# An attention, 2-D DFT and MLP kernel: the DFT as 6- and 4-point elementwise DFTs with small tile DFTs behind them, and the three stages of different batches interleaved by a hand-written dispatcher

## The chip, the core and the metric

One Trainium2 chip, one of its cores. The metric is device time in microseconds of one execution. The core has five engines that run in parallel, each through its own instructions in order: PE (matrix products, with weight loads, PEld, beside them), DVE (vector), ACT (activations), POOL (GpSimd) and SP, which here only issues DMAs. PE writes to PSUM, eight banks of 2 KB a partition; everything else lies in SBUF (128 partitions) or in DRAM.

## The reference

```python
# q, k, v: (4, 8, 768, 64) f32; n_global = 8, n_local = 96; w_ch1: (512, 2048); w_ch2: (2048, 512)
scores = matmul(q, k.T) / sqrt(64)                   # per batch and head
keep = (key < n_global) | (0 <= query - key < n_local)
dist = n_local where a global key is not local, else |query - key|
scores = where(keep, scores - slope[head] * dist, -1e9)
x = softmax(scores) @ v                              # -> (4, 768, 512), the heads side by side
u = x + real(fft2(x))                                # over the sequence (768) and the channels (512)
un = (u - mean(u)) / sqrt(var(u) + 1e-6)             # over the channels
out = u + maximum(un @ w_ch1, 0) @ w_ch2
```

## The kernel before

A batch is 768 rows of 512 channels, so six tiles of 128 rows. The work of one batch has three stages, in f16 with f32 sums:

- `attention(b, hp)`, for a pair of heads: six DMAs bring q, k, v (`qsb`, `ksb`, `vsb`; 192 KB each, in rows of 256 bytes) in f32. ACT casts q and v, DVE casts k. PE transposes q and k tile by tile (`ptq`, `ptk`), DVE copies each (`qT`, `kT`). For each head and each tile of 128 keys, PE makes the scores `pss` (keys on partitions; 768 queries for the first tile, since its first 8 keys are seen by all, 256 for the others), ACT takes exp to `eraw`, and DVE multiplies by a mask in f16, `b0m` or `bgm`, which holds the exponentials of the distance and zeros, and which DMAs bring. For each tile of queries, PE sums up to three products (`pav`) with v and a column of ones, DVE takes the reciprocal of the last column (`rcol`), and ACT or DVE scales to `xn`.
- `mix(b)`, first part: the DFT over the sequence as a full product with cosine and sine matrices (`csm`, `ssm`): for four tiles of channels and two matrices, six products of 512 columns to `pm`; DVE copies (`yt`) and fills the last 256 columns by symmetry. Then the DFT over the channels: for each of six row tiles, eight products of 512 columns to `pmx`. DVE adds `xn` to give `u` and takes its statistics (`st`, `mvall`); after the sixth tile ACT and DVE make one `rstd` for all; DVE normalises (`un`), PE transposes (`ptu`), DVE copies (`unT`).
- `mix(b)`, second part, the MLP, in two halves of 384 rows: 16 times four products to `ph`, with the relu on ACT (`hT`); then for three row tiles 16 products of 512 columns to `pg`; DVE adds `u` (`ob`), a DMA writes it.

The weights come in f32 through a single staging buffer each (`w1tmp`, `w2tmp`), and DVE casts them. The order is that of the program at its end: attention of batch 0, the loads of constants and weights, and then for each batch the attention of the next one and the mix of this one. A scheduler orders the instructions on each engine by their data and their buffers, with that order as the priority; the pools (`bufs`) set how far a stage runs ahead. PSUM is split into three banks for attention, three for mix and MLP, two for transposes.

Of the kernel before, what the change touches and what calls it, by code (L numbers as in the profile page):

```python
# [9 lines left out]
FP16 = mybir.dt.float16  # L11
# [4 lines left out]
P = 128  # L16

CAST_E = "scalar"
MASK_E = "gpsimd"
# [3 lines left out]
def kernel(  # L23
# [19 lines left out]
    HP = H // 2  # L43

    hsl = np.arange(H, dtype=np.float64)
    slopes = 2.0 ** (-8.0 * (hsl + 1) / H)

    kk = np.arange(P)[:, None]
    qq = np.arange(256)[None, :]
    rel_g = qq - kk  # L50
    in_band_g = (rel_g >= 0) & (rel_g < NL)
    Bgen = np.zeros((H, P, 256))
    for h in range(H):
        Bgen[h] = np.where(in_band_g, np.exp(-slopes[h] * rel_g), 0.0)
    qa = np.arange(S)[None, :]
    rel0 = qa - kk
    in_band0 = (rel0 >= 0) & (rel0 < NL)
    is_g = kk < NG
    dist0 = np.where(in_band0, rel0, NL)
    B0 = np.zeros((H, P, S))  # L60
    for h in range(H):
        loc = np.where(in_band0, np.exp(-slopes[h] * rel0), 0.0)
        glob = np.exp(-slopes[h] * dist0)
        B0[h] = np.where(is_g, glob, np.where(kk >= NG, loc, 0.0))
    b0_d = nc.inline_tensor(B0.astype(np.float16), name="b0m")
    bg_d = nc.inline_tensor(Bgen.astype(np.float16), name="bgm")

    ii = np.arange(S)
    ang_s = 2.0 * np.pi * np.outer(ii % S, ii) / S
    CS = np.cos(ang_s)  # L70
    SSm = np.sin(ang_s)
    ddi = np.arange(Dm)
    ang_d = 2.0 * np.pi * np.outer(ddi, ddi) / Dm
    CD = np.cos(ang_d)
    SDn = -np.sin(ang_d)
    cs_d = nc.inline_tensor(CS.astype(np.float16), name="csm")
    ss_d = nc.inline_tensor(SSm.astype(np.float16), name="ssm")
    cd_d = nc.inline_tensor(CD.astype(np.float16), name="cdm")
    sd_d = nc.inline_tensor(SDn.astype(np.float16), name="sdm")
    id_d = nc.inline_tensor(np.eye(P, dtype=np.float16), name="idm")  # L80

    konst = ctx.enter_context(tc.tile_pool(name="konst", bufs=1))
    att = ctx.enter_context(tc.tile_pool(name="att", bufs=2))
    att1 = ctx.enter_context(tc.tile_pool(name="att1", bufs=2))
    mixp = ctx.enter_context(tc.tile_pool(name="mixp", bufs=1))
    up = ctx.enter_context(tc.tile_pool(name="up", bufs=1))
    outp = ctx.enter_context(tc.tile_pool(name="outp", bufs=2))
    xnp = ctx.enter_context(tc.tile_pool(name="xnp", bufs=2))
    small = ctx.enter_context(tc.tile_pool(name="small", bufs=12))
    ps = ctx.enter_context(tc.tile_pool(name="ps", bufs=3, space=bass.MemoryType.PSUM))  # L90
    psm = ctx.enter_context(tc.tile_pool(name="psm", bufs=3, space=bass.MemoryType.PSUM))
    pst = ctx.enter_context(tc.tile_pool(name="pst", bufs=2, space=bass.MemoryType.PSUM))

    def cast_op(o, i, scale=None):
        if CAST_E == "scalar":
            if scale is None:
                nc.scalar.activation(o, i, AF.Copy)
            else:
                nc.scalar.activation(o, i, AF.Copy, 0.0, scale)
        else:  # L100
            if scale is None:
                nc.vector.tensor_copy(o, i)
            else:
                nc.vector.tensor_scalar_mul(o, i, scale)

    mask_ctr = [0]

    def mask_op(o, a, bm):
        eng = nc.gpsimd if (mask_ctr[0] % 2 == 0) else nc.vector
        mask_ctr[0] += 1  # L110
        eng.tensor_tensor(o, a, bm, op=ALU.mult)

    ident = konst.tile([P, P], FP16, tag="ident", name="ident")
    nc.sync.dma_start(ident, id_d.ap())
    epsc = konst.tile([P, 1], FP32, tag="epsc", name="epsc")
    nc.vector.memset(epsc, 1e-6)
    b0_sb = []
    bg_sb = []
    for h in range(H):
        t1 = konst.tile([P, S], FP16, tag=f"b0_{h}", name=f"b0_{h}")  # L120
        nc.sync.dma_start(t1, b0_d.ap()[h])
        b0_sb.append(t1)
        t2 = konst.tile([P, 256], FP16, tag=f"bg_{h}", name=f"bg_{h}")
        nc.sync.dma_start(t2, bg_d.ap()[h])
        bg_sb.append(t2)
    cs_sb = []
    ss_sb = []
    cd_sb = []
    sd_sb = []
    w1f = []  # L130
    w2f = []

    def load_big_consts():
      for a in range(NS):
          t1 = konst.tile([P, S], FP16, tag=f"cs{a}", name=f"cs{a}")
          nc.sync.dma_start(t1, cs_d.ap()[a * P:(a + 1) * P, :])
          cs_sb.append(t1)
          t2 = konst.tile([P, S], FP16, tag=f"ss{a}", name=f"ss{a}")
          nc.sync.dma_start(t2, ss_d.ap()[a * P:(a + 1) * P, :])
          ss_sb.append(t2)  # L140
      for a in range(ND):
          t1 = konst.tile([P, Dm], FP16, tag=f"cd{a}", name=f"cd{a}")
          nc.sync.dma_start(t1, cd_d.ap()[a * P:(a + 1) * P, :])
          cd_sb.append(t1)
# [219 lines left out]
```

## Time and profile before

| | |
|---|---|
| time, median of 3 runs | 450.07 us (449.8 to 451.08) |
| span of the profiled execution, its own time | 452.1 us |
| PE busy | 390.5 us, 86% of the span |
| DVE, ACT, POOL busy | 242.2, 199.5, 0.2 us |
| mean granted clock of PE | 0.913 |
| DMA | 39.52 MB, mean 87 GB/s |

The span runs from the first to the last instruction of one execution. Busy times of PE hold pipelined matmuls and overlap themselves. A group's row gives: line, engine, operation, out<-in, its shape and count | busy us, mean ns of one | idle time of the engine just before them, and what ended it. A row of the chain in order of time gives start, duration and what ran. In a row by stretches stand the stretch, its length, the busy time and count of PE, PEld, DVE, ACT and POOL, the granted clock, the share of the DMA engines, and GB/s.

### The profile page before, as it was taken

The numbers are of one execution on the slowest core, as the hardware profiler recorded it, in microseconds if no ns is written. First come the engines' busy times: TensorE is split into PE (matmuls) and PEld (weight loads), VectorE is DVE, ScalarE is ACT, GpSimd is POOL, SyncE is SP. The second block draws the span as 40 slices with busy tenths as digits, with TensorE's granted clock in tenths as the row PEclk, the third lists the DMA queues.
The fourth block names the chain that finished last, engine by engine and source line by source line (L and its number), as shares of the span: only waits on it lengthen the run. The fifth ranks groups of instructions, "written<-read, shape, count | busy, mean of one in ns | idle before, by whom it ended". The sixth has DMA issues, their size and how long they took to land.

```text
span 452.1 us, 6542 instructions
## 1 busy us (share of the span) xinstructions
PE 390.5 (86%) x2272; PEld 190.2 (42%) x2272; DVE 242.2 (54%) x1029; ACT 199.5 (44%) x506; POOL 0.2 (0%) x4
## 2 busy tenths in 40 slices
PE   0488989957889999999769999999589999959996
PEld 0133334323345454444335454444255554435452
DVE  0377678989872104898970104999950105871101
ACT  1377451548666150786716160776424330006060
POOL 0000000000000000000000000000000000000000
PEclk9999989955559999998959999999969999979999
DMA  7999318887799101362340101000000101000101
GB/s 205 223 223 304 78 35 225 250 222 195 175 199 164 70 1 70 71 129 56 81 88 0 71 0 71 0 3 1 1 0 7 65 25 46 1 0 1 60 11 71
DMA packets 87537, 39.52 MB, mean 87 GB/s; under 512 B 76752, under 2 KB 81360, under 8 KB 87504
## 3 DMA queue, kind: packets, MB, share of 16 engines
q1 hardware_dynamic: 87504, 39.10, 35.0%
q8 instruction: 18, 0.29, 0.3%
q14 instruction: 15, 0.12, 0.1%
HBM read 32.80 MB, written 6.29 MB: 86 GB/s over the span
## 4 chain that ended last, share of the span: by engine, by line
PE 73%; DVE 13%; DMA 7%; ACT 3%; issue 2%; SPq 1%; DVEq 0%; ACTq 0%
PE ph L306 20%; PE pg L315 18%; PE pm L261 9%; PE pmx L279 8%; PE pss L224 5%; PE pss L213 3%; PE pav L240 3%; DMA w2tmp<-in_moe_w_ch_dram 3%; PE ptk L197 2%; DVE un L292 2%; DMA w1tmp<-in_moe_w_ch_dram 2%; PE ptq L194 2%; PE ptu L297 2%; DVE rcol L243 2%; DVE expst L228 2%
## 5 line engine op out<-in xcount | busy, mean ns | idle before, releaser
L310 ACT ACTIVATE hT<-ph 128x384 f16<-128x384 f32 x128 | 62.7, 490 | 89.2 <-PE ph L306 87.9
L306 PE MATMUL ph<-unT,w1f 128*128 128x384 f16 x512 | 97.0, 344 | 0.0
L318 DVE TENSOR_TENSOR ob<-pg,u 128x512 f32<-128x512 f32 x24 | 16.6, 691 | 142.0 <-PE pg L315 142.0
L315 PE MATMUL pg<-w2f,hT 128*128 128x512 f16 x384 | 84.2, 379 | 0.0
L306 PEld LDWEIGHTS <-w1f 128*128 128x128 f16 x512 | 52.0, 102 | 39.4 <-issue 9.1
L315 PEld LDWEIGHTS <-hT 128*128 128x128 f16 x384 | 37.6, 98 | 44.4
L227 ACT ACTIVATE eraw<-pss 128x256 f16<-128x256 f32 (+1 forms) x160 | 49.0, 369 | 5.8 <-PE pss L224 4.1
L217 ACT ACTIVATE eraw<-pss 128x384 f16<-128x384 f32 x64 | 29.8, 489 | 46.6 <-PE pss L213 46.2
L240 PE MATMUL pav<-v,expst 128*128 128x65 f16 x480 | 41.7, 212 | 9.4 <-ACT xn L245 4.6
L240 PEld LDWEIGHTS <-expst 128*128 128x128 f16 x480 | 32.0, 108 | 29.8 <-issue 12.4
L224 PE MATMUL pss<-qT,kT 64*128 64x256 f16 (+1 forms) x160 | 41.5, 307 | 2.1 <-ACT eraw L217 1.3
L245 ACT ACTIVATE xn<-pav,rcol 128x64 f16<-128x64 f32 x96 | 28.7, 311 | 31.3 <-DVE rcol L243 30.7
L297 PE MATMUL ptu<-ident,un 128*128 128x128 f16 x96 | 24.2, 280 | 18.5 <-DVE un L292 13.6
L194 PE MATMUL ptq<-ident,q 128*128 128x128 f16 x96 | 24.0, 250 | 18.5 <-ACT q L181 16.8
L228 DVE TENSOR_TENSOR expst<-eraw,bg 128x256 f16<-128x256 f16 (+1 forms) x160 | 36.4, 272 | 4.4 <-ACT eraw L227 3.1
L261 PE MATMUL pm<-cs,xn 128*128 128x512 f16 x96 | 30.3, 416 | 0.0
L243 DVE RECIPROCAL rcol<-pav 128x1 f32<-128x1 f32 x192 | 26.5, 161 | 6.8 <-PE pav L240 4.3
L197 PE MATMUL ptk<-ident,k 128*128 128x128 f16 x96 | 23.8, 248 | 6.5 <-DVE kT L198 5.5
L279 PE MATMUL pmx<-sd,yt 128*128 128x512 f16 x96 | 29.2, 385 | 0.0
L279 PE MATMUL pmx<-cd,yt 128*128 128x512 f16 x96 | 28.8, 391 | 0.0
L261 PE MATMUL pm<-ss,xn 128*128 128x512 f16 x96 | 26.6, 385 | 0.8 <-DVE yt L265 0.8
L188 ACT ACTIVATE v<-vsb 128x384 f16<-128x384 f32 x32 | 16.7, 521 | 22.8 <-DMA vsb<-in_v_dram 18.3
(35 smaller groups left out, 337.8 us busy)
## 6 DMA issues: line engine op xcount, KB each, us to landing
qsb<-in_q_dram SPq DMA_DIRECT2D x32, 192.0 KB, 4.1
ksb<-in_k_dram SPq DMA_DIRECT2D x32, 192.0 KB, 4.2
vsb<-in_v_dram SPq DMA_DIRECT2D x32, 192.0 KB, 4.2
out_dram<-ob SPq DMA_DIRECT2D x24, 256.0 KB, 2.0
w1tmp<-in_moe_w_ch_dram SPq DMA_DIRECT2D x8, 512.0 KB, 4.3
w2tmp<-in_moe_w_ch_dram SPq DMA_DIRECT2D x16, 256.0 KB, 3.4
b<-b0m SPq DMA_DIRECT2D x8, 192.0 KB, 3.5
cs<-csm SPq DMA_DIRECT2D x6, 192.0 KB, 4.0
```

The source lines that it names most:

```text
L194: nc.tensor.transpose(pt, q16[:, i * P:(i + 1) * P], ident)
L224: nc.tensor.matmul(pss, kT[hb:hb + Dh, i * P:(i + 1) * P], qT[hb:hb + Dh, qlo:qlo + w], start=True, stop=True)
L227: nc.scalar.activation(eraw[:, ecol(i):ecol(i) + w], pss, AF.Exp)
L228: nc.vector.tensor_tensor(expst[:, ecol(i):ecol(i) + w], eraw[:, ecol(i):ecol(i) + w], bg_sb[h][:, 0:w], op=ALU.mult)
L240: nc.tensor.matmul(pav[:, 0:65], lhsT, v16b[hslot][:, kb, 0:65], start=(t == 0), stop=(t == n - 1))
L243: nc.vector.reciprocal(rcol, pav[:, 64:65])
L261: nc.tensor.matmul(pm, xn[b][si][:, dc * P:(dc + 1) * P], kon[si][:, 0:512], start=(si == 0), stop=(si == NS - 1))
L279: nc.tensor.matmul(pm, yt[(ch, di)][:, j * P:(j + 1) * P], kon2[di], start=(t == 0), stop=(t == 2 * ND - 1))
L297: nc.tensor.transpose(ptu, un16t[j][:, dc * P:(dc + 1) * P], ident)
L306: nc.tensor.matmul(ph, w1f[di][:, jb * P:(jb + 1) * P], unTt[di][:, half * 384:(half + 1) * 384], start=(di == 0), stop=(di == ND - 1))
L310: nc.scalar.activation(hT, ph, AF.Relu)
L315: nc.tensor.matmul(pg, hTt[jb][:, jj * P:(jj + 1) * P], w2f[jb], start=(jb == 0), stop=(jb == NJ - 1))
```

## The change

The kernel is written anew, in one file of 774 lines.

- **DFT over the sequence, 768 = 6 x 128.** `u_fold_s` takes a 6-point DFT over the six row tiles, elementwise on DVE, for each half of the channels, to six combinations `z`. **DFT over the channels, 512 = 4 x 128.** `u_fold_d` does the same with a 4-point DFT over the four tiles of channels (`ww`). What is left are 128-point DFTs with twiddles: `u_y` (`py`, 24 products of 256 columns a batch) over the sequence, and `u_u` (`pu`, six times eight products of 128 columns) over the channels. Only half of the combinations are made; the others are mirrored copies (`rev`, reversed in the free dimension), on POOL. Rows now come out in the order row = 6 m + r, so x is written to DRAM and read back in that order (`xd`, `xr`) for the sum, and the output is written in it.
- **Attention.** The first 8 keys are split off: all score tiles are 256 or 128 wide, and the global keys of four heads are one product (`u_glob`, `pgl`) with their values gathered in `vG` (`pvg`). The two heads of a pair stand side by side: four score products in a row, alternately for rows 0 to 63 and 64 to 127, and one DVE instruction masks both. Six transposes share one bank and one copy of 768 columns. `pav` holds four heads, with one reciprocal and one scaling on DVE. The masks `mk` are made on the chip from one table of distances (ACT exp, eight times). v is cast on POOL.
- **Normalisation.** rstd is made on POOL (`pow`) for three tiles at a time, `un`, `ptu`, `unT` follow for three tiles.
- **Loads.** q and k of batch 0 go to the buffers that later hold `hT`; of later batches, a pair of heads is issued when v of the pair before is cast. The weights are eight DMAs from POOL, straight to f16, with no staging.
- **Order.** The scheduler is off (`manual_schedule`). A dispatcher keeps a clock for each engine with assumed costs, and picks at each step among three lists (attention and mix of a batch, `A`; `ph`; quarters of `pg`) the piece that could start first. `flex` puts a copy on ACT or DVE, whichever this clock has free first. PSUM: five banks for all of A (`x`), two for `ph`, one for `pg`.

```diff
-        for ch in range(2):
-            ...
-                    nc.tensor.matmul(
-                        pm, xn[b][si][:, dc * P:(dc + 1) * P],
-                        kon[si][:, 0:512],
-                        start=(si == 0), stop=(si == NS - 1))
-        ...
-        for j in range(NS):
-            ...
-                    nc.tensor.matmul(pm, yt[(ch, di)][:, j * P:(j + 1) * P],
-                                     kon2[di], start=(t == 0),
-                                     stop=(t == 2 * ND - 1))
+    def u_fold_s(b, half):
+        ...
+            lo, hi = x[:, 0:3, c0:c0 + cw], x[:, 3:6, c0:c0 + cw]
+            VT(ab[:, 0], lo, hi, op=ALU.add)
+            VT(ab[:, 1], lo, hi, op=ALU.subtract)
+            VT(pm[:, 0], ab[:, :, 1], ab[:, :, 2], op=ALU.add)
+            VT(pm[:, 1], ab[:, :, 1], ab[:, :, 2], op=ALU.subtract)
+            zc = z[:, :, c0:c0 + cw]
+            VT(zc[:, 0], ab[:, 0, 0], pm[:, 0, 0], op=ALU.add)
+            VT(zc[:, 1], ab[:, 1, 0], pm[:, 1, 1], op=ALU.subtract)
+            nc.vector.scalar_tensor_tensor(zc[:, 2], pm[:, 0, 0], -0.5, ab[:, 0, 0], op0=ALU.mult, op1=ALU.add)
+            nc.vector.scalar_tensor_tensor(zc[:, 3], pm[:, 1, 1], 0.5, ab[:, 1, 0], op0=ALU.mult, op1=ALU.add)
+            nc.vector.tensor_scalar_mul(zc[:, 4], pm[:, 1, 0], c)
+            nc.vector.tensor_scalar_mul(zc[:, 5], pm[:, 0, 1], c)
+    def u_fold_d(b):
+        ...
+            VT(eg[:, 0], z[:, :, 0:256], z[:, :, 256:512], op=ALU.add)
+            VT(eg[:, 1], z[:, :, 0:256], z[:, :, 256:512], op=ALU.subtract)
+            VT(ww[:, 0:6], e0[:, :, 0:128], e0[:, :, 128:256], op=ALU.add)
+            VT(ww[:, 6:12], e0[:, :, 0:128], e0[:, :, 128:256], op=ALU.subtract)
+            VT(ww[:, 12:14], F[:, 2:4], Hh[:, 4:6], op=ALU.add)
+            ...
+    def u_y(b, n):
+        ...
+                nc.tensor.matmul(o, wr, t1_sb[:, rs, 128:384], start=True, stop=(wi is None))
+                if wi is not None:
+                    nc.tensor.matmul(o, wi, t1_sb[:, rs, 0:256], start=False, stop=True)
+            ...
+            end = flex(0.62, 0.68, e,
+                       lambda: nc.scalar.activation(dst, src, AF.Copy),
+                       lambda: nc.vector.tensor_copy(dst, src))
+    def mirror(b, end):
+        ...
+        for n in range(3, 7):
+            nc.gpsimd.tensor_copy(rev[:, n - 2], y[:, n, :, :, ::-1])
+    def u_u(b, rs):
+        ...
+                for c in range(2):
+                    nc.tensor.matmul(o, yy[:, c, :], t2_sb[:, rd, (0 if c == 0 else (2 if mir else 1)), :],
+                                     start=(c == 0), stop=(c == 1))
+            ...
+            VT(u.rearrange("p (n r) -> p r n", r=4), pu.rearrange("p (r n) -> p r n", r=4),
+               XR[b][:, rs, :].rearrange("p (n r) -> p r n", r=4), op=ALU.add)
+            nc.vector.bn_stats(st, u)
+            nc.vector.bn_aggr(mv[:, rs % 3, :], st)
+            if rs % 3 == 2:
+                nc.gpsimd.tensor_scalar_add(rs_t, mv[:, :, 1], 1e-6)
+                nc.gpsimd.tensor_tensor(rs_t, rs_t, mhalf[:, 0:3], op=ALU.pow)
+    def u_av(b, half, j):
+        ...
+            if half == 1 and j == NS - 1:
+                nc.sync.dma_start(xd.rearrange("(j p) d -> p j d", p=P), X[b])
+                nc.sync.dma_start(xr, xd.rearrange("(m r) d -> m r d", r=6))
-      for a in range(NJ):
-          tmp = konst.tile([P, Dm], FP32, tag="w2tmp", name=f"w2tmp{a}", bufs=1)
-          nc.sync.dma_start(tmp, moe_w_ch2[a * P:(a + 1) * P, :])
-          ...
-          nc.vector.tensor_copy(t, tmp)
+    def load_w():
+        for a in range(4):
+            nc.gpsimd.dma_start(w1[:, :, a * 512:(a + 1) * 512],
+                                moe_w_ch1[:, a * 512:(a + 1) * 512].rearrange("(c p) f -> p c f", p=P))
+        ...
+    def mix(b):
+        u = [u_fold_s(b, 1), u_fold_d(b)]
+        u += [u_y(b, n) for n in range(len(YP))]
+        u += [u_u(b, rs) for rs in order]
+        u += [u_u(b, 3)] + [u_n(b, 0), u_n(b, 1), u_n(b, 2)]
+        u += [u_nt(b, 0), u_u(b, 4), u_nt(b, 1), u_u(b, 5), u_nt(b, 2)]
+        u += [u_n(b, 3), u_n(b, 4), u_n(b, 5), u_nt(b, 3), u_nt(b, 4), u_nt(b, 5)]
-    for b in range(B):
-        if b + 1 < B:
-            for hp in range(HP):
-                attention(b + 1, hp)
-        mix(b)
+        A = [x for b in range(B) for x in att(b) + mix(b)]
+        PH = [u_ph(c, jb) for c in range(2 * B) for jb in range(NJ)]
+        PGU = [u_pg(c, t, part) for c in range(2 * B) for t in range(3) for part in range(5)]
+        while ia < len(A) or ip < len(PH) or ig < len(PGU):
+            ...
+                gate = 32 * (b - 1) - 3 + r * 30.0 / K
+                if t is not None and (b == 0 or ip >= gate or ip == len(PH)):
+                    cands.append((max(t - 0.2, now), 0, "A"))
+            ...
+            which = min(cands)[2]
```

More of the change, by code (lines that the diff above doesn't have):

```diff
@@ L55 @@
[L55 to L79, printed above, removed]
@@ L106 @@
[L106 to L125, printed above, removed]
```

759 lines of the change are left out of this document (554 added, 205 removed).

## The prediction

> **What bounds the kernel now.** I read the page first: the engines' totals, the granted clock by slice, and the shares of the chain that ended last.
>
> ```profile
> span 452.1 us, 6542 instructions
> PE 390.5 (86%) x2272; PEld 190.2 (42%) x2272; DVE 242.2 (54%) x1029; ACT 199.5 (44%) x506; POOL 0.2 (0%) x4
> PEclk9999989955559999998959999999969999979999
> PE 73%; DVE 13%; DMA 7%; ACT 3%; issue 2%; SPq 1%; DVEq 0%; ACTq 0%
> ```
>
> PE carries 73% of the chain, and POOL does nothing. Busy PE time overlaps itself, so prices come from the chain in order of time, where a dense run shows what one matmul adds.
>
> ```profile
> 133.19 1.28 PE ph L306 x4
> 155.91 10.40 PE ph L306 x64
> 166.31 10.36 PE pg L315 x48
> 376.32 10.36 PE pm L261 x48
> 386.68 10.37 PE pmx L279 x48
> 35.52 0.49 PE pav L240 x9
> 448.37 0.69 DVE ob L318
> ```
>
> One MLP half costs 10.40 + 10.36 = 20.76 us, the eight 166.1 us. The two DFT products of one batch cost 20.73 us, 82.9 us for four. A column costs 10.36/(48 x 512) = 0.42 ns; a 65-column matmul costs 0.49/9 = 54 ns, which I take as the floor for every small one. The first MLP product stands only at 133.19: until then the kernel loads, and does attention 0, attention 1 and mix 0. So there are two things to cut: DFT work, and the time before the first `ph`.
>
> Next, what happens where PE waits. Stretches of 2 us around the normalisation of batch 2 (columns: busy PE, PEld, DVE, ACT, POOL with counts, granted clock, DMA share, GB/s):
>
> ```profile
> 322.00:324.00 2.00, 0.50 (x3) 0.01 (x1) 2.00 (x8) 1.80 (x3) 0.00 (x0) 1.00 0.01 4
> 324.00:326.00 2.00, 0.00 (x0) 0.00 (x0) 2.00 (x6) 0.00 (x0) 0.00 (x0) 1.00 0.00 0
> 326.00:328.00 2.00, 0.40 (x2) 0.24 (x3) 1.56 (x6) 0.30 (x1) 0.00 (x0) 0.65 0.00 0
> 334.00:336.00 2.00, 2.00 (x11) 1.27 (x10) 1.06 (x5) 0.49 (x1) 0.00 (x0) 0.50 0.00 0
> 336.00:338.00 2.00, 2.00 (x13) 1.19 (x11) 0.67 (x3) 0.98 (x2) 0.00 (x0) 0.79 0.00 0
> ```
>
> DVE is full while PE waits some 4 us for `u` and its statistics, and then the granted clock is 0.5 for about 10 us, also under dense `ph` at 334.
>
> **The change, part by part.** Durations of the trace that the new instructions are priced by:
>
> ```profile
> L227 ACT ACTIVATE eraw<-pss 128x256 f16<-128x256 f32 x128 | 42.7, 391 | 5.3 <-PE pss L224 4.1
> L217 ACT ACTIVATE eraw<-pss 128x384 f16<-128x384 f32 x64 | 29.8, 489 | 46.6 <-PE pss L213 46.2
> L181 ACT ACTIVATE q<-qsb 128x768 f16<-128x768 f32 x16 | 13.5, 841 | 5.8 <-DMA qsb<-in_q_dram 3.4 <-PE ptq L194 2.3
> L188 ACT ACTIVATE v<-vsb 128x384 f16<-128x384 f32 x32 | 16.7, 521 | 22.8 <-DMA vsb<-in_v_dram 18.3 <-PE pav L240 4.4
> L228 DVE TENSOR_TENSOR expst<-eraw,bg 128x256 f16<-128x256 f16 x128 | 31.5, 285 | 4.1 <-ACT eraw L227 3.1
> L219 DVE TENSOR_TENSOR expst<-eraw,b 128x768 f16<-128x768 f16 x32 | 17.7, 553 | 3.8 <-ACT eraw L217 3.3
> L265 DVE CAST yt<-pm 128x512 f16<-128x512 f32 x32 | 21.9, 686 | 5.3 <-PE pm L261 5.3
> L285 DVE BATCH_NORM_STATS2 st<-u 128x6 f32<-128x512 f32 x24 | 16.3, 684 | 0.2
> L283 DVE TENSOR_TENSOR u<-pmx,xn 128x512 f32<-128x512 f32 x24 | 16.0, 676 | 1.2 <-PE pmx L279 0.8
> L286 DVE BATCH_NORM_AGGREGATE mvall<-st 128x2 f32<-128x6 f32 x24 | 4.1, 171 | 0.2
> L292 DVE TENSOR_SCALAR un<-u,mvall,rstd 128x512 f16<-128x512 f32 x24 | 12.7, 538 | 0.1
> L243 DVE RECIPROCAL rcol<-pav 128x1 f32<-128x1 f32 x192 | 26.5, 161 | 6.8 <-PE pav L240 4.3
> L269 DVE TENSOR_SCALAR yt<-yt 128x256 f16<-128x256 f16 x16 | 3.6, 222 | 0.2
> ```
>
> From 285 ns at 256 and 553 at 768, an f16 `TENSOR_TENSOR` takes 0.151 us + 0.52 ns an element; from 391 and 489, an exp takes 0.195 us + 0.77 ns (480 columns: 0.56). One output tile of attention (a reciprocal and a product of 256 from PSUM, 0.15 + 256/512 x (0.686 - 0.15) = 0.42) is 0.58. `u_fold_s`: 2 x 0.55 + 2 x 0.42 + 2 x 0.285 + 2 fused ones at the slow rate (0.42) + 2 x 0.22 = 3.8. `u_fold_d`: 2 x 0.95 + 2 x 0.55 + 4 x 0.285 = 4.15. One `u` with its statistics: 0.676 + 0.684 + 0.171 = 1.53.
>
> *PE work.* Of one batch, in us: q/k transposes 48 x 0.054 = 2.6; scores 10,752 columns = 4.5 (15,360 before); attention times v 88 x 0.054 + 8 x 0.11 = 5.6 (120 x 0.054 = 6.5 before); global keys 0.9 + 0.4; `py` 24 x 256 columns = 2.6; `pu` 48 x 0.054 = 2.6; `ptu` 1.3; sum 20.5, where the DFT part is 5.2 instead of 20.7. After the first `ph` there remain eight MLP halves (166.1), three batches (61.6) and half a `ptu` set (0.6): 228.3. The scores of two heads now stand in a row on partitions 0-63 and 64-127; before has no such neighbours, so what the second costs is unknown: all of it (0 saved) or nothing (3 x 4.5/2 = 6.8 saved). No row is nearer to one of these; I take the middle, 224.9.
>
> *The start.* The order in which q, k, v and the weights are issued moves. Before, SP brings the weights after all of batch 0 and the constants, through one staging buffer at a time (`w1tmp`, `w2tmp`) and a cast on DVE:
>
> ```order
> L146 DMA sd_982<-sdm 128x512
> L152 DMA w1tmp_0_985<-in_moe_w_ch_dram 128x1024
> L157 DMA w2tmp_1012<-in_moe_w_ch_dram 128x512
> L177 DMA qsb_0_1076<-in_q_dram 128x6x64
> L177 DMA ksb_0_1077<-in_k_dram 128x6x64
> L177 DMA vsb_0_1078<-in_v_dram 128x6x64
> L152 DMA w1tmp_1_988<-in_moe_w_ch_dram 128x1024
> ```
>
> Now POOL issues them as eight large DMAs, between its casts of v for the second and the third pair of heads (`vs_1`, `vs_2`):
>
> ```order
> L636 COPY mk<-mk 128x2x224 x4
> L191 CAST v_79<-vs_0_93 128x6x2x64
> L226 COPY kG_81<-kT_0_175 64x8 x2
> L191 CAST v_79<-vs_1_102 128x6x2x64
> L652 DMA w_72<-in_moe_w_ch_dram 128x4x512 x4
> L656 DMA w_73<-in_moe_w_ch_dram 128x4x512 x4
> L226 COPY kG_81<-kT_1_238 64x8 x2
> L191 CAST v_79<-vs_2_110 128x6x2x64
> L226 COPY kG_81<-kT_2_293 64x8 x2
> L191 CAST v_79<-vs_3_117 128x6x2x64
> ```
>
> The weights leave the staging buffers and DVE, and now run beside the last third of batch 0.
>
> ```profile
> 8.71 0.50 SPq L177 DMA_DIRECT2D qsb<-in_q_dram  x1
> 23.55 0.84 SPq L177 DMA_DIRECT2D vsb<-in_v_dram  x1
> 22.60:33.90 11.30, 9.17 (x56) 4.33 (x56) 8.26 (x45) 8.17 (x25) 0.00 (x0) 1.00 1.15 223
> 33.90:45.20 11.30, 9.67 (x61) 4.25 (x60) 8.75 (x48) 8.61 (x25) 0.00 (x0) 1.00 0.94 304
> ident<-idm SPq DMA_DIRECT2D x1, 32.0 KB, 1.8
> out_dram<-ob SPq DMA_DIRECT2D x24, 256.0 KB, 2.0
> ```
>
> Batch 0 is 24 transfers of 192 KB in 256-byte rows. At 223 GB/s that is 21.2 us, with the first landing (0.7 + 1.8) and two small constants 1.0: 24.7. Before, 2.3 MB of constants stood ahead (first q issued at 8.71); they go, and eight exps on ACT (0.59 each, hidden under the loads) build the masks. PE's order has `pvg`, which needs all four v casts, ahead of the scores of pair 2, so the last v holds up everything behind it. Its cast moves to POOL: no row; ACT took 2 x 0.52, and I take 1.0. The weights are 8.4 MB, at 304 GB/s 27.6 us. They start near 16 (mask exps from about 7.5 to 12, then four copies and two casts on POOL), when 1.85 MB of q, k, v are missing, 8.3 us alone. Two queues at once are not in the trace: the delay is 0 (they don't hinder) to 27.6 (weights first); I take equal shares, 8.3, as nearest to a rate that is simply split.
>
> From the last v to the first `ph`, on one path: `pvg` and its copy 0.9; ACT's 12 exps and one 768 copy 8 x 0.56 + 4 x 0.49 + 0.84 = 7.3; last mask product and `x` 1.6; DVE then 3.8 (first fold) + 6 x 0.58 + 3.8 + 4.15 = 15.2; 24 `py` at half clock, as PE has waited, 5.2, and their last copy 1.1; four `u` 6.6 with the wait for `pu`; three `un` 1.6; `ptu`, copy and hand-overs 1.2 and 0.8. Sum 41.5. The write and read back of x through DRAM (two transfers of 786 KB, at 304 GB/s 2.6 each plus 2.0 to land, 9.2) lie beside the second fold onwards (3.8 + 4.15 + 6.3); without that cover they would be 9.2 on the path. First `ph`: 24.7 + 1.0 + 8.3 + 41.5 = 75.5, against 133.2.
>
> *The mix of batches 1 to 3.* Before, DVE ends the statistics of all six tiles, then normalises and copies in quarters:
>
> ```order
> L285 BN_STATS st_1_5_3381<-u_5_159 128x6
> L286 BN_AGGR mvall_3305<-st_1_4_3368 128x2
> L182 CAST k_3_0_3820<-ksb_0_3811 128x768
> L286 BN_AGGR mvall_3305<-st_1_5_3381 128x2
> L189 MEMSET v_3_0_0_3823 128x6
> ```
>
> Now three tiles' rstd come from POOL, and `un` stands behind the fourth `u` and behind `ob`:
>
> ```order
> L495 TENSOR_TENSOR u_2_1639<-pu_2_1630,xr_1480 128x4x128
> L503 BN_STATS st_2_1641<-u_2_1639 128x6
> L504 BN_AGGR mv_0_1612<-st_2_1641 128x2
> L495 TENSOR_TENSOR u_3_1656<-pu_3_1647,xr_1480 128x4x128
> L503 BN_STATS st_3_1659<-u_3_1656 128x6
> L504 BN_AGGR mv_3_1658<-st_3_1659 128x2
> L603 TENSOR_TENSOR ob_2_1669<-pg_2_1591,u_5_751 128x512
> L523 TENSOR_SCALAR un_0_1672<-u_0_1610,mv_0_1612,rstd_2_1644 128x512
> ```
>
> PE's order there is `pg` x16, `pg` x16, `py` x24, `pg` x9, `pu` x32, `pg` x7, `ptu`. Between `pu_0` and `ptu_0` DVE needs 4 x 1.53 + 0.69 + 0.54 = 7.4 and its hand-overs; PE has four `pu` and 7 `pg`, 3.2, so it waits 4.8. Before that, the second `pg` waits for the only `pg` bank, whose `ob` stands behind the fold (0.58 + 3.8 + 0.69 against 3.45), and `py` for the second fold: 2.6. Then `unT` of the third tile 1.25, and the second half's `un` 0.85. Together 9.5 a batch, 28.5 in all; ends 20 (hand-overs free, pauses partly under others) and 36. A pause of 4.8 halves the clock as at 326; 5 us of dense `ph` at half rate lose 2.5 a batch, 7.5; ends 0 and 15. Elsewhere PE and attention interleave as here:
>
> ```profile
> 282.50:305.10 22.60, 21.75 (x160) 9.78 (x160) 20.57 (x105) 17.48 (x52) 0.00 (x0) 1.00 0.00 1
> ```
>
> 3.8% idle, of about 43 us in three batches 4.9. ACT and DVE there need less than PE: some 31 and 26 us. Mirrored copies, v casts and rstd on POOL are hidden, the mirrors behind `u` (6.1 us). The tail is `ob` 0.69, its landing 2.0, issue 0.3: 3.0.
>
> *Sum:* 75.5 + 224.9 + 28.5 + 7.5 + 4.9 + 3.0 = 344.3 us of span. The span before is 2.0 over the median of the runs, 450.07, so the time is 342.
>
> **The rivals.**
> Better: the weights don't hinder (-8.3), the score pairs overlap (-3.4), the clock holds (-7.5): 323. For it: 1.00 in the row at 282.5, beside interleaved work. Against it: the 0.50 rows.
>
> Weights first: +19.3, 362. For it: their rows are 2 KB against 256 bytes. At 223 and 304 GB/s over 16 engines such packets take 18 and 108 ns, so that alternating packets leave q, k, v 15% of the time, and the weights are through first. The Trainium skill (DMA: Bandwidth & Descriptors, Queues, rings and completion order) has just this rule, turns at packet granularity; no run here shows it.
>
> POOL and DVE hold each other up: POOL's 4 casts and 5 large mirrors a batch, 1 us each, are 9 us; if half of it lengthens DVE where it is late, 4.5 x 4 = +18, 360. The Trainium skill (SBUF — State Buffer, Who interferes with whom) speaks for it: GpSimd and VectorE share one port pair as an exclusive lock, which a VectorE instruction with two SBUF inputs takes too. By it the folds and mask products would be hit, `u` and `y` (PSUM) not; with POOL idle, no row of before can agree or disagree.
>
> Slower than before: a mirrored copy of 512 elements on POOL costs far more than 1 us. Four stand in a row ahead of rstd and of `pu_4`, with a cover of about 6 us. Each batch then loses 4t - 6; to eat the 108 us saved, t must reach 8.2 us.
>
> ```profile
> L267 DVE COPY yt<-yt 128x256 f16<-128x256 f16 x16 | 3.5, 219 | 0.1
> ```
>
> On DVE, such a reversed copy takes 0.22 us for 256; 8.2 for 512 would be some 19 times as slow.
>
> **How the numbers follow.** Forecast 0.47, better 0.22, weights first 0.15, POOL against DVE 0.12, slower 0.03, rest 0.01. The low ends together (-8.3, -3.4, -8.5, -7.5, -4.9) give 310 and the high ends of one or two terms 380; the range 308 to 380 leaves out about 2 in 10 on both sides, mostly above. About 0.3% is what a measurement of this kernel can tell. Faster 0.96, the same 0.01, slower 0.03.
>
> **What would show it.** First `ph` near 75; between v's last landing and it DVE nearly full; `w1` DMAs landing while v of pair 3 is late. `py` and `pu` together near 5 us a batch. In the mixes pauses of PE of 4 to 5 us ahead of `ptu_0`, released by DVE `un`, and the clock at 0.5 after it. POOL near 40 us of work in all. Wrong: a first `ph` past 95, a reversed POOL copy over 2 us, POOL as releaser of `pu` or `un`, or DVE and not PE filling the stretches of attention beside MLP.

## The result and the profile after

| kernel | time, us (median) | ratio to before, 95% interval | span, us | mean clock |
|---|---|---|---|---|
| before | 450.1 | 1 | 452.1 | 0.913 |
| changed | 359.3 | 0.797 [0.795, 0.800] | 357.4 | 0.960 |

Executions more than 1.5% longer than the fastest of the same kernel are left out of every median; one of them, of 694.9 us, was the profiled one of the kernel with heads not alternating below, so that this kernel was run twice.

The changed kernel takes 90.8 us less. The forecast was 342: right in direction, and 17 us too low. The totals and the chain's shares of the changed kernel:

```profile
span 357.4 us, 5463 instructions
PE 272.4 (76%) x2100; PEld 155.5 (44%) x2100; DVE 210.5 (59%) x470; ACT 142.6 (40%) x282; POOL 51.5 (14%) x113
PE 57%; DVE 22%; SPq 8%; DMA 7%; issue 2%; POOL 2%; ACT 1%; POOLq 0%; DVEq 0%
```

PE fell from 390.5 to 272.4 us of busy time. DVE's share of the chain rose from 13% to 22%, and SP's queue, which was next to nothing, has 8%: a stretch of loads now ends late. The chain in order of time shows where (start, duration, what), and a view of the tile `ph` gives its first and last start:

```profile
25.86 20.27 DMA vs<-in_v_dram
...
46.29 0.83 POOL v L191
...
353.06 0.69 DVE ob L603
```

```profile
L569 PE MATMUL ph<-unT,w x512: 322/326/524, 87.0 to 342.0; 128*128 128x384 f16 x171
```

The last transfer of v, 192 KB, took 20.27 us to land. The first `ph` starts at 87.0 instead of 133.2, and from there to the end there are 270.4 us instead of 318.9: the change took 46.2 us out of the start of the profiled span and 48.5 out of the rest. The rest by stages (the stretch, its length, busy PE, PEld, DVE, ACT, POOL, clock, DMA share, GB/s); attention beside MLP alternates with mix:

```profile
87.02:93.00 5.98, 4.65 (x33) 2.62 (x33) 4.43 (x9) 2.96 (x6) 1.91 (x3) 1.00 0.00 0
93.00:134.60 41.60, 41.60 (x360) 22.44 (x358) 25.92 (x62) 26.62 (x56) 4.39 (x11) 1.00 0.61 128
134.60:166.00 31.40, 22.59 (x169) 14.06 (x166) 26.35 (x52) 6.03 (x12) 6.08 (x12) 0.89 0.26 84
166.00:208.00 42.00, 41.87 (x362) 22.77 (x361) 25.99 (x64) 27.59 (x57) 4.03 (x11) 1.00 0.64 126
208.00:240.00 32.00, 23.92 (x166) 14.55 (x165) 26.25 (x52) 6.42 (x12) 6.08 (x12) 0.89 0.27 82
240.00:282.50 42.50, 42.10 (x363) 22.84 (x362) 26.29 (x64) 27.53 (x57) 3.95 (x11) 1.00 0.49 97
282.50:314.00 31.50, 23.11 (x167) 14.36 (x166) 25.89 (x52) 6.53 (x12) 5.29 (x11) 0.89 0.27 85
```

In the stretches from 93.0, 166.0 and 240.0, attention stands beside MLP and leaves PE idle for 0.0, 0.1 and 0.4 us; each mix leaves it idle for 8.8, 8.1 and 8.4 us. PE's waits (in all, times, longest) say for what:

```profile
PE ptu L545 <- DVE un L523: 28.1, 8, 6.9
PE pvg L262 <- POOL v L191: 23.0, 1, 23.0
PE pg L598 <- DVE ob L603: 2.6, 3, 1.1
```

There is one wait of 23.0 us for the last v of batch 0, and there are eight for the normalisation, `ptu` for `un`. The groups that the prediction priced:

```profile
L495 DVE TENSOR_TENSOR u<-pu,xr 128x512 f32<-128x512 f32 x24 | 25.4, 1057 | 8.4 <-PE pu L490 8.4
L462 POOL COPY rev<-y 128x512 f16<-128x512 f16 x16 | 9.1, 615 | 0.0
L509 POOL TENSOR_TENSOR rstd<-rstd,mhalf 128x3 f32<-128x3 f32 x8 | 7.1, 882 | 0.7
```

### The profile page after: what moved, and what is told of

Its sections match the earlier page's. It is cut to its first block, busy times and chain, and to the rows that moved or that the text cites. A ratio compares the mean times of both kernels' runs of the same rounds, so it can differ in the third digit from the quotient of the medians.

```text
span 357.4 us, 5463 instructions
## 1 busy us (share of the span) xinstructions
PE 272.4 (76%) x2100; PEld 155.5 (44%) x2100; DVE 210.5 (59%) x470; ACT 142.6 (40%) x282; POOL 51.5 (14%) x113
## 4 chain that ended last, share of the span: by engine, by line
PE 57%; DVE 22%; SPq 8%; DMA 7%; issue 2%; POOL 2%; ACT 1%; POOLq 0%; DVEq 0%
PE pg L598 21%; PE ph L569 19%; DMA vs<-in_v_dram 7%; SPq L176 7%; DVE u L495 7%; DVE st L503 5%; PE pav L324 4%; PE sc L241 3%; DVE ob L603 2%; PE py L429 2%; DVE un L523 2%; PE ptu L545 2%; PE pav L313 2%; PE pu L490 2%; PE py L432 1%
## 5 line engine op out<-in xcount | busy, mean ns | idle before, releaser
L569 PE MATMUL ph<-unT,w 128*128 128x384 f16 x512 | 97.9, 329 | 2.7 <-ACT unT L549 2.7
L598 PE MATMUL pg<-w,hT 128*128 128x512 f16 x384 | 94.3, 379 | 3.3 <-DVE ob L603 2.6
L569 PEld LDWEIGHTS <-w 128*128 128x128 f16 x512 | 48.2, 99 | 42.2 <-issue 10.0
L250 DVE TENSOR_TENSOR ex<-er,mk 128x960 f16<-128x960 f16 (+1 forms) x48 | 31.8, 665 | 40.4 <-ACT er L246 40.2
L246 ACT ACTIVATE er<-sc 128x480 f16<-128x480 f32 (+1 forms) x96 | 45.9, 556 | 8.1 <-PE sc L241 6.4
L495 DVE TENSOR_TENSOR u<-pu,xr 128x512 f32<-128x512 f32 x24 | 25.4, 1057 | 8.4 <-PE pu L490 8.4
L441 ACT ACTIVATE y<-py 128x512 f16<-128x512 f32 x16 | 9.2, 596 | 40.2 <-PE py L432 39.9
L332 DVE TENSOR_TENSOR x<-pav,rc 128x256 f16<-128x256 f32 x48 | 20.4, 425 | 1.6
L241 PE MATMUL sc<-qT,kT 64*128 64x256 f16 x192 | 19.0, 290 | 2.9 <-ACT q L200 2.1
L324 PE MATMUL pav<-v,ex 128*128 128x65 f16 x352 | 20.6, 207 | 0.0
L324 PEld LDWEIGHTS <-ex 128*128 128x128 f16 x352 | 15.2, 105 | 8.2 <-issue 4.4
L503 DVE BATCH_NORM_STATS2 st<-u 128x6 f32<-128x512 f32 x24 | 16.7, 695 | 0.8
L523 DVE TENSOR_SCALAR un<-u,mv,rstd 128x512 f16<-128x512 f32 x24 | 13.1, 599 | 5.3 <-POOL rstd L509 5.3
```

Source lines behind the costliest of these rows:

```text
L241: nc.tensor.matmul(pa[s][:, c0:c0 + w], kT[lo:lo + 64, i * P:(i + 1) * P], qT[lo:lo + 64, i * P:i * P + w], start=True, stop=True)
L246: nc.scalar.activation(er[:, s, 0:n], pa[s][:, 0:n], AF.Exp, 0.0, 0.125)
L250: nc.vector.tensor_tensor(expst[hp][:, :, g * 512:g * 512 + n], er[:, :, 0:n], mk[:, 2 * hp:2 * hp + 2, m0:m0 + n], op=ALU.mult)
L324: nc.tensor.matmul(o, lhsT, v16[b % 2][:, i, h, 0:65], start=(j < 2 and a == 0), stop=(a == len(ops) - 1), skip_group_check=True)
L495: VT(u.rearrange("p (n r) -> p r n", r=4), pu.rearrange("p (r n) -> p r n", r=4), XR[b][:, rs, :].rearrange("p (n r) -> p r n", r=4), op=A ...
L503: nc.vector.bn_stats(st, u)
```

## The experiments

All are edits of the changed kernel. Differences are to its 359.3 us; the ratio is to the kernel before, which was run again beside each group of experiments and had medians from 450.1 to 454.1 us. A difference of about 3 us is therefore not certain from the times alone, and there the traces have to bear it out. For this the stretch from the first to the last `ph` helps, 87.0 to 342.0 in the changed kernel, 255.0 us.

**The weights later.** `load_w` is called after the fourth v cast.

```diff
-                if not wload and ia == 12:
+                if not wload and ia == 25:
```

> The weight transfers are issued from POOL only after v of the fourth pair of heads of batch 0 has been cast (piece 25 of the list instead of piece 12). Theory A (weights first): in the changed kernel the last v landed at 46.1 where its share of 223 GB/s would have brought it near 25, so q, k and v should be through near 25 to 27, the first ph should move from 87.0 to near 67, and the time fall by about 20 us, to near 339. The weights then have from about 27 to 67 for 8.4 MB, 27.6 us at 304 GB/s, so w1 should still be in time. Theory B (bytes are the limit, whichever goes first): the last v early, but w1 then lands late and the first ph waits for it, so that the time falls by less than 5 us. Theory C (the wait for v lies beside work that is needed anyway): no change within 1 us.

Measured: 343.3 us, ratio 0.761 [0.759, 0.764], 16.0 less. In the chain of this run, v lands at once, and another transfer is late:

```profile
20.45 4.41 DMA vs<-in_v_dram
...
42.92 10.63 DMA xd<-x
53.57 5.10 DMA xr<-xd
```

and among its waits:

```profile
DVE u L495 <- DMA xr<-xd: 5.6, 1, 5.6
```

The same transfer lands in 4.41 us, at 24.9 instead of 46.1. The first `ph` moved from 87.0 to 70.8, not to 67: the write of x now runs beside the weights and takes 10.63 us, and DVE waits 5.6 us for `xr`. Theory A holds but for this, B and C fall. The DMA queues over 4 us show how the weights hold up v (packets, MB, and the time of the packets as a share of 16 engines; the software queue has the weights, the hardware queue q, k and v): the changed kernel from 26 to 30, then this run from 12 to 16, where no weights run.

```profile
q0 software_dynamic: 625, 0.62, 91.4%
q1 hardware_dynamic: 625, 0.16, 29.9%
```

```profile
q1 hardware_dynamic: 3507, 0.87, 136.2%
```

Beside the weights both queues move the same number of packets, and those of v, which are a quarter of the size in these counts, bring 0.16 MB where 0.87 passed alone.

**The weights in two parts.** `w1` at the same place, `w2` behind the read back of x.

```diff
-                if not wload and ia == 12:
-                    load_w()
+                if ia == 25:
+                    load_w1()
+                if ia == IW2:      # all py of batch 0 ordered
+                    load_w2()
```

> As the first run with late weights, but only the first MLP weight is issued there; the second is issued when the products py of batch 0 have been ordered, behind the write and read back of x. Theory A (in the first run the weights' second half ran beside the read back of x, for which the first u of batch 0 then waited 5.6 us): this wait goes, the first ph comes near 70.5 instead of 76.1, and the time falls by another 5 to 6 us, to near 338. Theory B (the read back is late by itself, or the second weight then comes too late for pg): no gain on 343.3, or a loss.

(The 76.1 in this text is not the first `ph` of the run with late weights, but the first long piece of them in its chain; the first is the 70.8 above.) Measured: 338.5 us, ratio 0.751 [0.748, 0.754], another 4.8 less, with the first `ph` at 64.9, 5.9 earlier, and no wait for `xr`. Theory A holds. Together the place of the weights costs 20.8 us.

**The sum u without a strided write.** (Strided means that neighbouring elements of the result do not stand side by side in memory.) u stays in the order of its products, `w1` is loaded in that order, and `ob` reads u with a stride.

```diff
-            VT(u.rearrange("p (n r) -> p r n", r=4), pu...
+            VT(u.rearrange("p (r n) -> p r n", r=4), pu...
-                nc.vector.tensor_tensor(ob, pg, UT[(b, rs)], op=ALU.add)
+                VT(ob.rearrange("p (n r) -> p n r", r=4), pg...,
+                   UT[(b, rs)].rearrange("p (r n) -> p n r", r=4), op=ALU.add)
```

> The sum u is kept in the channel order in which its product comes out, so that its DVE instruction writes contiguous elements and no longer strided ones; the first MLP weight is loaded in the same order of channels, and the last sum ob reads u strided instead. Theory A (the strided write makes it 1057 ns instead of the 676 ns of the kernel before): u falls to some 700 to 850 ns; four of them stand on the path of each mix, two or so more in its second half, so each batch gains 1.5 to 2.3 us, all four 6 to 9, and ob grows by up to 0.4 us but lies beside PE work except for the last one: the time falls by 5 to 9 us, to near 352. Theory B (the strided read of PSUM and of x is what costs): u stays near 1050 ns and the time within 1 us, or up to 3 us slower by ob.

Measured: 355.3 us, ratio 0.787 [0.784, 0.790], 4.0 less. The two groups in this run:

```profile
L495 DVE TENSOR_TENSOR u<-pu,xr 128x512 f32<-128x512 f32 x24 | 16.1, 669 | 9.1 <-PE pu L490 9.1
L603 DVE TENSOR_TENSOR ob<-pg,u 128x512 f32<-128x512 f32 x24 | 24.7, 1029 | 37.7 <-PE pg L598 37.6
```

u is back at 669 ns, although it still reads x with a stride of four elements: the strided write was the cost, as theory A has it, with less gain than its 5 to 9 us. `ob`, which now reads with a stride of 128 elements, rose from 688 to 1029 ns and took part of the gain back: PE's waits of `pg` for `ob` rose from 2.6 to 5.9 us in all. From the first to the last `ph` there are 250.0 us, 5.0 less, but the first came 1.1 us later, at 88.1, with a longer wait for the last v.

**The stride on PE instead.** `pu` writes its columns with a stride of four into PSUM; u and `ob` have none.

```diff
-                o = pu[:, rd * P:(rd + 1) * P]
+                o = pu.rearrange("p (n r) -> p r n", r=4)[:, rd, :]
```

> The products pu write their 128 columns with a stride of four elements into the PSUM bank, so that the sum u reads PSUM and x and writes u without a stride, and ob too (in the run with the permuted u, ob grew from 692 to 1032 ns). Theory A (PE writes with a stride as fast): u takes about 0.67 us instead of 1.06, pu stays near 54 ns a product, ob stays at 0.69, and the time falls by 5 to 7 us, more than the 4.0 with the permuted u. Theory B (a strided write costs PE as it cost DVE): pu grows by half or more, and the gain is below 3 us or gone.

Measured: 356.2 us, ratio 0.788 [0.782, 0.793], 3.1 less. u takes 0.67 us, but 22 products in a row, of the changed kernel first and then of this run (start, duration), show what it costs PE:

```profile
147.57 1.39 PE L490 MATMUL pu<-t,y 128*128 128x128 f16 x22
```

```profile
221.56 2.61 PE L490 MATMUL pu<-t,y 128*128 128x128 f16 x22
```

The granted clock was 1.00 in both places. PE takes nearly twice as long to write with the stride, so theory B is right on the mechanism, and the gain is at its limit of 3; from the first to the last `ph` it is 3.7 (87.9 to 339.2). The Trainium skill (SBUF — State Buffer, Door 1: The DMA port swizzle) says that non-contiguous access to PSUM slows matmuls, and that four float32 may be stepped over for free in SBUF: the trace agrees on PSUM and on the read of x, and does not on the write of u.

**Four times the DFT products.** Each `py` and `pu` is issued four times.

```diff
-                for c in range(2):
+                for c in (0, 1, 0, 1, 0, 1, 0, 1):
```

> Every product of py and pu is issued four times into the same bank, which leaves the result as it is and brings PE's DFT work back from some 5.2 to 20.7 us a batch, as it was before the change. Theory A (PE's work counts one for one): three times 5.2 us in each of four batches, +62, and at the start at half clock some more: 415 to 430. Theory B (the sums u on DVE pace the products of pu, so that three more of each are covered there): only py and part of pu count, +30 to +40: 390 to 400.

Measured: 403.8 us, ratio 0.894 [0.891, 0.898], 44.5 more, between the two theories.

```profile
L495 DVE TENSOR_TENSOR u<-pu,xr 128x512 f32<-128x512 f32 x24 | 25.7, 1069 | 26.7 <-PE pu L490 26.7
```

u now waits 26.7 us for `pu` instead of 8.4, and the pause ahead of `ptu_0` of the second batch falls from 6.0 to 2.1 us. From that `ptu_0` to the next batch's there are 85.5 us (177.72 to 263.20) instead of 73.9 (156.84 to 230.78): of 15.5 us more of PE work in a batch, 4 went into the pause that was there, and 11.6 count. The smaller DFT products are thus worth some 45 us here.

**No interleaving.** A batch begins when the MLP of the one before is issued.

```diff
-                gate = 32 * (b - 1) - 3 + r * 30.0 / K
-                if t is not None and (b == 0 or ip >= gate or ip == len(PH)):
+                if t is not None and ip >= 32 * b and ig >= 30 * b:
```

> Attention and mix of batch b start only when all MLP work of batch b-1 has been issued (the rest of the dispatcher as it is). Theory A (the hand order covers the waits of attention and mix with MLP products): attention alone is then paced by ACT and DVE, as in batch 0, where it took some 25 us beyond the loads with PE mostly waiting, and the pauses of the mix have no pg in them; each of three batches loses 14 to 17 us, +42 to +50, to 400 to 410. Theory B (PE has the same work in any order, and its queue runs ahead far enough): within 10 us of the changed kernel.

Measured: 460.7 us, ratio 1.020 [1.017, 1.024], 101 more. Both theories miss. The two stretches from the last MLP product of batch 0 into the first of batch 1, which start at 194.8:

```profile
133.98:153.90 19.92, 7.46 (x56) 4.02 (x57) 8.07 (x13) 9.44 (x18) 4.10 (x9) 0.57 1.21 216
153.90:200.10 46.20, 29.12 (x250) 18.82 (x250) 37.28 (x88) 13.73 (x26) 6.49 (x15) 0.63 0.20 50
```

In the first, q, k and v are loaded, as their transfers are issued with the casts of the pair before and so were held back too: the edit took away more than the interleaving. In the second, DVE is busy for 37 of 46 us and PE runs at a clock of 0.63. To separate the loads, the first eight pieces were let through:

```diff
-                if t is not None and ip >= 32 * b and ig >= 30 * b:
+                if t is not None and ((ip >= 32 * b and ig >= 30 * b) or (r < 8 and ip >= 32 * b - 16)):
```

> As the kernel without interleaving, but the first eight pieces of each batch (the casts of the first two pairs of heads and the transposes of the first, with which the loads of the next pairs are issued) may run beside the second MLP half of the batch before. In the run without them each batch began with 20 us (133.98 to 153.9) in which the DMA share was 1.21 at 216 GB/s and the last v landed at 153. Theory A (of the 101 us lost there, some 3 x 13 are loads that came late, and the rest, some 60, is attention and mix paced by DVE and a slow PE without MLP products in between): the time falls by 35 to 45 us, to 416 to 426. Theory B (attention alone needs these 20 us anyway, and the loads lie beside it): within 10 us of 460.7.

Measured: 439.6 us, ratio 0.969 [0.957, 0.981]: 21 less, where 35 to 45 were expected. In this run too, SP's queue issues half of q, k and v of batch 1, 12 of 24 transfers, only from 138.95 to 148.2, behind the MLP of batch 0, which ended near 134. So only the other half was let ahead. Neither theory holds. Some 80 us remain as the worth of the interleaving, a bound from above, since loads are still in it.

**Dummy products in the pause.** 24 products of 512 columns ahead of the first `ptu`.

```diff
+            if rs == 0:
+                for _ in range(24):
+                    nc.tensor.matmul(wb, idn, w2[:, 0, :], start=True, stop=True)
```

> Ahead of ptu of each half's first tile of a batch, PE does 24 more products of 512 columns into a bank that nobody reads (only the first half has them: 5.0 us in each of four batches), in the time in which it waited for un. Theory A (the half clock after the pause costs what the prediction took, 2.5 us a batch): the granted clock stays at 1.0 there, and the time falls by 5 to 7 us. Theory B (the slow work after the pause is covered, or the clock falls in any case): within 1 us. Theory C (the 5.0 us don't fit into the pause, since they come after pu_3 and hold back ptu): slower by up to 4 us, above all in batch 0.

Measured: 362.1 us, ratio 0.801 [0.798, 0.805], 2.8 more. PE in the same place of batch 1 (start, duration; in brackets the idle time before), in the changed kernel and then in this run:

```profile
156.84 0.61 PE L545 MATMUL ptu<-ident,un 128*128 128x128 f16 x4 [6.04 <-DVE un L523]
...
164.69 1.31 PE L545 MATMUL ptu<-ident,un 128*128 128x128 f16 x12 [0.89 <-DVE un L523]
165.84 1.46 PE L569 MATMUL ph<-unT,w 128*128 128x384 f16 x8
```

```profile
156.44 0.40 PE L549 MATMUL ptu<-ident,un 128*128 128x128 f16 x4 [0.90 <-DVE un L523]
...
163.87 1.52 PE L549 MATMUL ptu<-ident,un 128*128 128x128 f16 x12 [2.16 <-DVE un L523]
165.19 2.77 PE L573 MATMUL ph<-unT,w 128*128 128x384 f16 x8
```

```profile
166.00:168.00 2.00, 2.00 (x10) 1.01 (x8) 0.88 (x2) 0.10 (x2) 0.00 (x0) 0.50 0.23 53
```

The clock holds through the pause (`ptu` 0.40 instead of 0.61 us). But DVE is no earlier with the second half, so PE then waits 2.16 us instead of 0.89, and the half clock comes after that, under dense `ph` (2.77 us for eight instead of 1.46, in the last row at a clock of 0.50). From one batch's `ptu_0` to the next there are 75.0 us (156.44 to 231.47) instead of 73.9. In batch 0, where the clock also fell in the pause, the first `ph` comes 1.4 us earlier, at 85.6, but from the first to the last there are then 259.3 us, 4.3 more. So the fall of the clock was moved to where it costs more; in the changed kernel it lies beside DVE's work. None of the three theories had this mechanism.

**v cast on ACT.** For batches 1 to 3.

```diff
-                    nc.gpsimd.tensor_copy(dst, src)
+                    nc.scalar.activation(dst, src, AF.Copy)
```

> The casts of v of batches 1 to 3 move from POOL (868 ns, 12 of them) to ACT. Theory A (POOL and DVE hold each other up): DVE's un and its mask products, which took 1.94 us for three un beside such a cast against 1.44 otherwise, get back 0.3 to 0.5 us for each cast, and where DVE is late the time falls by 1 to 3 us. Theory B (no such hold-up that counts): within 0.7 us, or slower by up to 2 us since ACT, which makes hT and the exps, has some 0.8 us more in each.

Measured: 364.1 us, ratio 0.806 [0.802, 0.810], 4.8 more. The three `un` of a second half, beside a POOL cast in the changed kernel, and without one in this run:

```profile
237.53 1.94 DVE L523 TENSOR_SCALAR un<-u,mv,rstd 128x512 f16<-128x512 f32 x3 [1.32 <-POOL rstd L509]
```

```profile
242.82 1.46 DVE L523 TENSOR_SCALAR un<-u,mv,rstd 128x512 f16<-128x512 f32 x3 [1.32 <-POOL rstd L509]
```

DVE gets back 0.48 us in such a place, as theory A has it, but the casts cost ACT 7 us in all (149.5 busy instead of 142.6), and a batch takes 1.5 us more (75.5 from one `ptu_0` to the next, 160.58 to 236.07, instead of 73.9). The dispatcher also ordered other work differently with these costs, so the 4.8 is not the cast's alone. Neither theory had a loss of this size. The casts' hold on DVE is thus small in the changed kernel. The mirrored copies were not moved, but the trace shows them: the first u of batch 1 runs beside one and takes 1.11 us, the next three, without, take 1.05, 1.03 and 1.03.

**Heads not alternating**, run twice.

```diff
-            for i, c0, w in ((2 * g, 0, 256), (2 * g + 1, 256, n1)):
-                for s in range(2):
+            for s in range(2):
+                for i, c0, w in ((2 * g, 0, 256), (2 * g + 1, 256, n1)):
```

> The four score products of a step are issued head after head, so that neighbours stand on the same 64 rows of PE and no longer on rows 0-63 and 64-127 in turn; everything else is unchanged. Theory A (neighbours on different rows overlap in part): in the changed kernel four products of 960 columns in all took 0.31 us where 0.42 ns a column gives 0.405; they go back to 0.40, and of 48 such steps 36 lie in the batches where PE sets the time, so the time grows by 36 x 0.09 = 3.2 us, 2 to 4. Theory B (the short time is a matter of how ends are modelled, and each product costs its columns): 0.31 us in the trace or not, the time stays within 0.7 us.

> The kernel of the run with the heads not alternating once more, for a profile. Theory A (products on different rows overlap): a step of 960 columns takes 0.40 us and each stretch of attention beside MLP grows by some 1 us. Theory B (they don't, or what they save is lost elsewhere): 0.31 us in a row as before, or 0.40 us in a row with the idle time of PE smaller by as much, and the stretches of the same length.

Measured: 360.0 us, ratio 0.797 [0.793, 0.801], and 358.9 in the single execution of the second time. In this order the rows change once in a step, where they changed three times. A step in the changed kernel, with a group of `ph` and `pg` ahead of it for comparison, and then a step in the second run:

```profile
112.67 0.81 PE L569 MATMUL ph<-unT,w 128*128 128x384 f16 x4
113.32 0.81 PE L598 MATMUL pg<-w,hT 128*128 128x512 f16 x3
...
114.85 0.81 PE L569 MATMUL ph<-unT,w 128*128 128x384 f16 x4
115.60 0.38 PE L241 MATMUL sc<-qT,kT 64*128 64x256 f16 x4
115.91 0.82 PE L598 MATMUL pg<-w,hT 128*128 128x512 f16 x3
```

```profile
114.66 0.81 PE L569 MATMUL ph<-unT,w 128*128 128x384 f16 x4
115.41 0.38 PE L241 MATMUL sc<-qT,kT 64*128 64x256 f16 x4
115.72 0.82 PE L598 MATMUL pg<-w,hT 128*128 128x512 f16 x3
```

From the first score product to what follows there is 0.31 us in both orders, and the stretches are equally long: theory B. The 0.31 us is also no saving against 0.405. Four `ph` ahead of `pg` last 0.65 us from start to start, but 0.75 ahead of the scores; with these 0.10 us a step costs 0.41, and 960 columns at 0.42 ns are 0.40.

**All that helped, together.** Weights in two parts, u in its own order, and in batch 0 the scores of the third pair and two output tiles ahead of the last v:

```diff
+        if b == 0:
+            u += [s2[0], a0[0], s2[1], a0[1], s2[2]] + T(3)[:3] + [u_vg(b)]
```

> Together: the weights in two parts, u in the permuted order (contiguous writes), and in batch 0 the scores of the third pair and two output tiles ahead of the casts of the fourth pair and of the product that gathers the global values, so that less of PE's work stands behind the last v. If the savings add up: -16 (late weights), -5.5 (read back of x), -4 (u), and up to -4 for the order in batch 0 (PE waited 4.1 us for the last v in the run with late weights): 359.3 - 29.5 = 330, range 328 to 336. If they cover each other (the last v early, DVE then paces batch 0 in any order): 334 to 338.

Measured: 330.4 us, ratio 0.733 [0.729, 0.736], 28.9 under the changed kernel, with the first `ph` at 63.1. That is close to the 29.5 that the expectation adds up. The weights and u account for 24.8 of it by their own runs; the order in batch 0 had no run of its own, and the first `ph` came 1.8 us earlier than with the weights alone.

## Why the prediction came out as it did

*The delay by the weights is the step that failed.* It is 13.1 of the 17 us. The sum took equal shares, a delay of 8.3 us. v landed at 46.1 instead of the 33.0 of the sum (24.7 + 8.3), and at 24.9 once the weights were behind it: the delay is 21.2, most of the 27.6 that "weights first" was worked out from. That rival gave 362 and had 0.15; the measured 359.3 stands beside it, and the first two experiments show its mechanism, though its first `ph` would have come at 94.8 (75.5 + 19.3) and came at 87.0. The choice of equal shares as "nearest to a rate that is simply split" was the error: the rows then at hand, packets of 18 and 108 ns, already gave q, k and v 15% of the time if packets alternate. The rule of the Trainium skill (DMA: Bandwidth & Descriptors, Queues, rings and completion order), turns at packet granularity, speaks for that outcome, and the trace agrees with it: 625 packets of each queue in 4 us, and 20.27 us beside the weights against 4.41. The equal counts are what turns packet by packet give; the order of single packets was not read.

*The load alone was right, and the chain to the first `ph` was right in its sum, in part by luck.* 24.7 was predicted for the landing, 24.9 measured without weights in the way. From the end of the last v cast to the first `ph` 41.5 was predicted, 39.9 measured (47.1 to 87.0), with parts that offset each other: to the first fold 10.6 for 9.8; the folds and six tiles 11.6 for 15.2, since the first `py` starts behind the first two sums of the last fold; `py` and its copy 5.7 for 6.3, with some 15 of the 24 products at half speed and not all; four u 7.7 for 6.6; from there on 4.4 for 3.6. The cast on POOL took 0.83 for 1.0. The read back of x stayed hidden; with late weights, where its write took 10.63 us, 5.6 us of it were not.

*From the first `ph` on, 268.8 predicted, 270.4 measured, with errors that cancel.* Idle PE was taken as 28.5 + 4.9 + 3.0 = 36.4. The rows by stages give 25.3 in the three mixes, 0.5 in attention, 1.3 in the last half of mix 0, and the last `ob` to the end is 4.3: 31.4. Work and half clock were taken as 224.9 + 7.5 = 232.4, and PE was then busy for the other 239.0. Of these 6.6, 3.4 is the overlap of score pairs that was taken off and that the run with heads not alternating shows is not there; the other 3 was not traced. That 268.8 came so near 270.4 is luck.

*From span to time, 4 us were lost.* The sum gave a span of 344.3, and the span measured is 357.4, which is the 13.1 of the late v; the other parts of the span cancel. The prediction then took 2 us off, because the profiled span of before lay 2.0 over the median time of other executions. In every execution whose span and time are both on record, the time is 1.7 to 2.8 us over the span, here 359.15 for 357.4.

*Inside the mix, three terms were mis-sized.* Sum u: 0.676 was taken from the unstrided row of before, and it took 1057 ns, 0.38 more each; four stand ahead of `ptu_0`, and the pause there was 6.0 and not 4.8. (Before, it was 5.1 in the trace, not "some 4".) Against that, `pg` waited for `ob` 2.6 us in the whole run, where 2.6 were taken a batch with the wait of `py`. The half clock appeared as predicted:

```profile
156.00:158.00 2.00, 1.16 (x12) 1.16 (x13) 2.00 (x5) 0.00 (x0) 0.00 (x0) 0.50 0.34 131
158.00:160.00 2.00, 2.00 (x19) 1.85 (x18) 1.65 (x3) 0.60 (x1) 0.00 (x0) 0.50 0.00 0
160.00:162.00 2.00, 1.31 (x8) 0.72 (x7) 1.93 (x4) 0.80 (x2) 0.00 (x0) 0.69 0.00 0
```

PE's work runs at it for some 4 us (from 156.8), but this is `ptu` and `pu` beside a DVE that is full, not the dense `ph` of the prediction, and PE's next wait, 0.89 us at 164.7, is for DVE again. In the run with dummy products PE was faster there and then waited longer. So most of the 7.5 us was a loss that DVE hides.

*The other rivals.* "Better" needed weights that don't hinder, which fell. POOL against DVE: 0.48 us where a cast stands beside three `un`, and under 0.1 where u stands beside mirrored copies, not 4.5 a batch. The Trainium skill (SBUF — State Buffer, Who interferes with whom) has these engines share a port pair, and counts `tensor_scalar` among what can take it; the 0.48 us on `un`, a `TENSOR_SCALAR`, agrees. What the folds lose was not tested. The slower case needed reversed copies of 8.2 us: they take 615 ns. POOL did 51.5 us of work, where 40 were expected, 7.1 of it for `pow`.

## What to carry to other kernels

A price per byte says nothing of who goes first: where two queues load at once, work out the bytes that each gets for the same number of packets, and start the transfer that nobody waits for behind the one that holds up the chain. A term worked out from a row holds only for the same access pattern: u cost 1057 ns where the row without a strided write said 676. Ahead of keeping PE warm, look at which engine ends the stretch: where DVE did here, PE's half clock cost little, and holding the clock gained nothing in all.

## What the hardware showed that was not expected

- A 192 KB transfer in 256-byte rows landed in 20.27 us beside 2 KB rows of another queue, and in 4.41 us without. In 4 us both queues moved 625 packets each.
- A float32 DVE sum of 512 elements: 669 ns with an operand read four elements apart, 1029 with one read 128 apart, 1057 with the result written four apart. PE writing 22 x 128 columns four apart into PSUM: 2.61 us instead of 1.39 at the same granted clock.
- The first 15 `py` of batch 0, after PE had been idle for 6.9 us, ran 0.21 us apart and the later ones 0.11, while the granted clock reads 1.00 in all these stretches: this reading alone does not show slow products.
- Half clock came after a pause of 6 us. With dummy work in that pause it came under the work that followed the next one, of 2.16 us; in the changed kernel that one was 0.89 us long, and the same work ran at full rate.
